# A sparse-attention and maxout-FFN kernel: the third output product of each half of the last FFN and the verdict's product use score tiles; the last product is made and stored in two column halves

## The chip, the cores and the metric

One core of one Trainium2 chip runs the program. The metric is the device time of one execution in microseconds; lower is better. Engine names are those of the profile: PE is the matrix engine's products, PEld its weight loads, DVE the vector engine, ACT the scalar engine, POOL the general-purpose engine, SP the engine whose queue issues most transfers. A "q" behind a name is that engine's sequencer or queue.

## The reference, cut to what matters

```python
# q, k, v: (4, 8, 768, 64); attention inside clusters, then a maxout FFN
mask   = q_assign[:, :, :, None] == k_assign[:, :, None, :]
attn   = softmax(where(mask, q @ k.T / sqrt(64), -1e9)) @ v
x      = attn.transpose(0, 2, 1, 3).reshape(3072, 512)
h      = maximum(maximum(x @ w1, x @ w2), x @ w3)      # 3072 x 768
return (h @ w_out).astype(float32)                     # 3072 x 512
```

## The kernel before, in words

There are 32 heads (4 batches of 8). Each head's tokens are sorted by cluster, its scores are made in blocks in a *score tile* (`big()`, line 69: two 512-column banks of the accumulator memory, in a pool of two buffers), its values in a *one-bank tile* (`one()`, line 72: 512 columns, a pool of two buffers), and the rows are gathered back into token order. The FFN of a batch of 768 tokens follows in two halves of 384 tokens (`ffn_units`, from line 923). A half has 18 hidden units (`hidden`, line 934), each 12 products of 384 columns into a one-bank tile at L941, evicted by ACT (L951) or DVE (L953), and after the third of a group cast by ACT (L957) and subtracted by DVE (L958) into a pair of 16-bit parts. Then come three output units (`outp(tt)`, tt = 0, 1, 2, line 963): 18 products of 512 columns at L974 into a one-bank tile, an eviction into an `o` tile of 128 x 512 (a tag `wd` of two buffers, line 982), and one store of it at L995 on SP's queue. In the last batch the eviction is by ACT for tt = 0 (L989), by DVE for tt = 1 (L987), and for tt = 2 ACT takes the left 256 columns (L992) and DVE the right 256 (L993), out of one bank.

The one-bank tiles are handed out to hidden units, output units, values and the verdict alike; score tiles to scores alone in the later batches. `judge` (line 1004) makes the verdict whether the sorted scheme may be used: some small vector operations, a product of 2 columns at L1015 into a one-bank tile, a reduction (L1017), a comparison (L1019), and `values_load` (L1020), which puts the flag into a register of every engine. At the program's end each engine branches on it (L1867): a second, general kernel runs only if the flag is set.

Order: every unit has a priority (its head number and an offset), `plan` lists the units by head, and the program is traced with `schedule_with_timeline_sim=True`: a planner orders each engine's queue by priority and by its own estimate of when operands are ready and buffers free. `judge` is put at priority `B * H - 0.5`, that is 31.5, the last scores at 31. The FFN of the last batch is traced last, all of its units with the same priority (`at_prio(B * H + 3, u)`). A queue executes in the order that the planner chose, and an instruction that waits holds up those behind it on its engine.

Of the kernel before, what the change touches and what calls it, by code (L numbers as in the profile page):

```python
# [14 lines left out]
AF = mybir.ActivationFunctionType  # L15
ALU = mybir.AluOpType
# [7 lines left out]
def sorted_attn__then__maxout_ffn(  # L24
# [17 lines left out]
    nc = tc.nc  # L42
    B, H, D, S = qk.shape
    D = D // 2
    C = cent.shape[0] // H
    P = 128
    QT = S // P
    NPAIR = H // 2
    DM = H * D
    DF = w1.shape[1]  # L50
    CT = DM // P
    JT = DF // P
    G = 3
    NB = G * P
    NG = QT // G
# [13 lines left out]
    def big():  # L69
        return ps_big.tile([P, 2 * 512], F32, tag="big", name="big")  # L70

    def one():
        return ps_one.tile([P, 512], F32, tag="one", name="one")

    def const(shape, dt, name):
        return cpool.tile(shape, dt, name=name)
# [7 lines left out]
    @contextmanager  # L84
    def behind(*made):
        with ExitStack() as s:
            for x in made:
                if x is not None:
                    s.enter_context(tc.issue_after(x.ins))
            yield  # L90
# [71 lines left out]
    for i, values in enumerate(SIDES.values()):  # L162
        x = 0
        while x < 4:
            n = 1
# [81 lines left out]
    wo16 = cpool.tile([P, JT, 2, DM], F16, name="wo16")  # L247
# [329 lines left out]
    def made(what, k):  # L577
        return st[k // H, k % H // 2][what, k & 1]
# [341 lines left out]
    HLS = ((0, 0), (0, 1), (1, 0))  # L920

    def ffn_units(b, gi):
        h16 = {}
        box = []
        tag = "wf" if gi else "vf"

        def slot(k):
            while len(box) <= k // 4:
                box.append(sb.tile([P, 4 * NB], F32, tag=tag, name=f"{tag}_h", bufs=2))
            return box[k // 4][:, k % 4 * NB : (k % 4 + 1) * NB]  # L930

        ms = {}

        def hidden(jt, i):
            def f():
                t = one()
                n = 0
                for ct in range(CT):
                    for xa, wa in HLS:
                        with behind(made("turn_pe", H - 1) if not (b or jt or i) else None):  # L940
                            nc.tensor.matmul(  # L941
                                t[:, 0:NB],
                                w16[:, jt, wa, i, ct],
                                x16[b, ct][:, xa * QT + gi * G : xa * QT + (gi + 1) * G, :],
                                start=(n == 0),
                                stop=(n == 3 * CT - 1),
                            )
                        n += 1
                m = slot(JT + (3 * jt + i) % 2)
                if i == 0:  # L950
                    nc.scalar.activation(m, t[:, 0:NB], AF.Copy, scale=2.0**-23)  # L951
                else:
                    nc.vector.scalar_tensor_tensor(m, t[:, 0:NB], 2.0**-23, ms[jt], op0=ALU.mult, op1=ALU.max)  # L953
                ms[jt] = m
                if i == 2:
                    x = slot(jt).bitcast(F16).rearrange("p (a n) -> p a n", a=2)
                    nc.scalar.copy(x[:, 0, :], m)  # L957
                    nc.vector.tensor_tensor(x[:, 1, :], m, x[:, 0, :], op=ALU.subtract)  # L958
                    h16[jt] = x

            return f

        def outp(tt):
            def f():
                if tt == 0:
                    so = ms["so"] = sb.tile([P, 1], F32, tag="so", name="so", bufs=3)
                    nc.vector.tensor_tensor(so, xsc[b][:, 0:1], wsc["w"], op=ALU.mult)
                    nc.vector.tensor_tensor(so, so, wsc["o"], op=ALU.mult)
                    nc.vector.tensor_scalar_mul(so, so, 2.0**9)
                t = one()  # L970
                n = 0
                for jt in range(JT):
                    for ha, wa in HLS:
                        nc.tensor.matmul(  # L974
                            t[:, 0:DM],
                            h16[jt][:, ha, tt * P : (tt + 1) * P],
                            wo16[:, jt, wa, :],
                            start=(n == 0),
                            stop=(n == 3 * JT - 1),
                        )  # L980
                        n += 1
                o = sb.tile([P, DM], F32, tag="wd", name="o", bufs=2)
                if b < B - 1:
                    nc.scalar.activation(o, t[:, 0:DM], AF.Copy, scale=ms["so"])
                elif tt < G - 1:
                    if tt & 1:
                        nc.vector.tensor_scalar(o, t[:, 0:DM], ms["so"], None, op0=ALU.mult)  # L987
                    else:
                        nc.scalar.activation(o, t[:, 0:DM], AF.Copy, scale=ms["so"])  # L989
                else:  # L990
                    h = DM // 2
                    nc.scalar.activation(o[:, 0:h], t[:, 0:h], AF.Copy, scale=ms["so"])  # L992
                    nc.vector.tensor_scalar(o[:, h:DM], t[:, h:DM], ms["so"], None, op0=ALU.mult)  # L993
                r = b * S + gi * NB + tt * P
                nc.sync.dma_start(out=out[r : r + P, :], in_=o)  # L995

            return f

        return [hidden(j, i) for j in range(JT) for i in range(3)] + [outp(tt) for tt in range(G)]
# [4 lines left out]
    def judge():  # L1004
        f = const([P, 2], F32, "flag_f")
        x = const([P, NH4], F32, "flag_x")
        v = nc.vector
        v.tensor_reduce(f[:, 0:1], n_off, axis=AX.X, op=ALU.max)
        v.tensor_scalar(x, n_key, float(C), None, op0=ALU.is_ge)
        v.scalar_tensor_tensor(x, n_own, 0.0, x, op0=ALU.is_equal, op1=ALU.mult)  # L1010
        v.tensor_reduce(f[:, 1:2], x, axis=AX.X, op=ALU.add)
        f16 = const([P, 2], F16, "flag_h")
        v.tensor_scalar(f16, f, 0.0, None, op0=ALU.is_gt)
        t = one()
        nc.tensor.matmul(t[0:1, 0:2], ones[:, 0:1], f16, start=True, stop=True)  # L1015
        r = const([1, 1], F32, "flag_r")
        v.tensor_reduce(r, t[0:1, 0:2], axis=AX.X, op=ALU.add)  # L1017
        bad = const([1, 1], I32, "bad")
        v.tensor_scalar(bad, r, 0.5, None, op0=ALU.is_ge)  # L1019
        verdict.append(nc.values_load(bad, min_val=0, max_val=1))  # L1020
# [15 lines left out]
    def when(p, k):  # L1036
        return p + AHEAD * max(0.0, 1.0 - (k - H) / H) if k >= H else p
# [3 lines left out]
    for b in range(B):  # L1041
        for hf in range(2):
            k = b * H + 4 * hf
            load, rest = four_units(b, hf)
            at = {H: 2, H + 4: H, 2 * H: H + 1}.get(k, max(k - 8, 0))
# [7 lines left out]
        for pr in range(NPAIR):  # L1053
            u = pair_units(b, pr)
            k = b * H + 2 * pr
            at = max(k - 5, 0)
            row_at = {H: 6, H + 2: 8, H + 4: 9, H + 6: 10}
            at = row_at.get(k, at)
            for x in u["load_rows"]:
                put(at, when(k - 5, k) - (k in (4, 6)), x)  # L1060
            at = max(k - 4, 0)
            at = row_at.get(k, at)
            for i, n in enumerate(("sums", "scales", "split_q")):
                put(at, when(k - 4 + 0.1 * i, k), u[n])
            for h in range(2):
                put(max(k + h - 4, at), when(k + h - 3.85, k), u["split_kv"][h])
                at, p = max(k + h - 2, 0), when(k + h - 2.5, k)
                if H <= k + h < H + 4:
                    at, p = H + 1, max(p, H + 0.7)
# [6 lines left out]
    for b in range(B):  # L1076
# [22 lines left out]
        if b + 1 < B:  # L1099
# [7 lines left out]
            units = hid + [u for x in units for u in x[3 * JT :]]  # L1107
            spread(units, k + 0.05, k + H, 0)
    put(B * H, B * H - 0.5, judge)
    spread(w_units(range(JT // 2)), 1, 6, 1)  # L1110
    spread(w_units(range(JT // 2, JT)), 9, 11.5, 0)
# [759 lines left out]
```

## Time and profile before

| | us |
|---|---|
| time before, median of 3 runs (lowest to highest) | 752.86 (752.25 to 754.35) |
| the profiled execution's own time | 747.1 |
| its span, first to last instruction | 745.3 |
| PE busy / DVE busy / ACT busy / POOL busy | 620.0 / 491.8 / 418.5 / 409.0 |

The profiled execution is 5.8 us below the median of the runs. The span starts at 0 and times in the rows count from there. The last FFN fills the stretch from about 642 us to the end; the verdict's product stands at 622.5 us. In a row of the timeline the first number is the start, the second the time from the first start to the last end of a run of like instructions, "x36" their count, and the bracket the idle time of the engine ahead of them with what ended it.

### The profile page before, as it was taken

To read this page: it belongs to the slowest core of one execution; us is meant where nothing else is said; L and a number is where in the kernel's file an instruction comes from. 1 tells how busy PE (TensorE), PEld (TensorE's weight loads), DVE (VectorE), ACT (ScalarE), POOL (GpSimd) and SP (SyncE) were. 2 spreads that over 40 slices of the span, in tenths; PEclk is the share of its full clock that TensorE was granted. 3 is DMA by queue.
4 is the path that set the end of the run, shared out by engine and by line. 5 is a ranking of instruction groups with operands and counts; after the bars stand their busy time and mean duration, and the time that the engine had idled before them with its cause. 6 is when DMAs were issued, how large, how long until landed. Compare 5 with 4: busy or idle time off the path is not lost.

```text
span 745.3 us, 12906 instructions
## 1 busy us (share of the span) xinstructions
PE 620.0 (83%) x4333; PEld 335.6 (45%) x4333; DVE 491.8 (66%) x1233; ACT 418.5 (56%) x1009; POOL 409.0 (55%) x426
## 2 busy tenths in 40 slices
PE   4556366467788986799999989998999999999995
PEld 1222233223444553365456555544555654564552
DVE  5898857779888999896759787853584532121220
ACT  5348978725869675666757578764565611211110
POOL 4576677735653777666664777766567555000000
PEclk8678878558899999999999999999999999999999
DMA  8864997889993995689785767665655644200001
GB/s 320 278 187 116 269 209 167 157 235 330 219 327 83 235 286 153 147 210 165 199 163 149 157 158 146 167 159 136 144 106 121 133 92 114 69 1 29 15 1 47
DMA packets 226908, 119.22 MB, mean 160 GB/s; under 512 B 196560, under 2 KB 205776, under 8 KB 226832
## 3 DMA queue, kind: packets, MB, share of 16 engines
q1 hardware_dynamic: 214928, 99.80, 54.5%
q0 software_dynamic: 11904, 18.50, 9.0%
q8 instruction: 36, 0.59, 0.3%
q14 instruction: 40, 0.33, 0.1%
HBM read 58.36 MB, written 28.84 MB: 117 GB/s over the span
## 4 chain that ended last, share of the span: by engine, by line
PE 42%; DMA 17%; issue 10%; POOL 10%; DVE 10%; ACT 9%; SPq 2%; DVEq 0%; POOLq 0%; ACTq 0%
PE one L941 22%; PE one L974 9%; POOL kv L692 6%; DMA pt<-hl 5%; POOL xb L848 4%; PE big L749 4%; DMA xb<-o,cl_idx 3%; ACT e L800 2%; DMA rows<-in_kr_dram 2%; DMA o<-of 1%; DVE kv L658 1%; DMA rows<-in_v_dram 1%; DVE hot L747 1%; DMA kv<-kv,cl_idx 1%; PE big L788 1%
## 5 line engine op out<-in xcount | busy, mean ns | idle before, releaser
L941 PE MATMUL one<-x,w 128*128 128x384 f16 x1728 | 296.8, 328 | 8.2 <-ACT wf_h L951 3.0
L692 POOL DMA_INDIRECT kv<-kv,cl_idx x192 | 206.9, 1077 | 115.8 <-issue 55.8
L848 POOL DMA_INDIRECT xb<-o,cl_idx x180 | 193.0, 1072 | 108.0 <-DMA o<-of 56.2
L941 PEld LDWEIGHTS <-w 128*128 128x128 f16 x1728 | 167.7, 98 | 122.9 <-issue 14.9
L749 PE MATMUL big<-hot,q 128*128 128x512 f16 x384 | 112.8, 410 | 30.2 <-DVE hot L747 20.4
L800 ACT ACTIVATE e<-big,nm,sc_al 128x128 f32<-128x128 f32 x256 | 113.4, 461 | 40.1 <-DVE nm L796 28.7
L747 DVE TENSOR_SCALAR hot<-line,cl_code 128x1024 f16<-128x1024 f16 x192 | 91.9, 500 | 12.8 <-PE big L749 12.4
L749 PEld LDWEIGHTS <-q 128*128 128x128 f16 x384 | 36.5, 103 | 75.4 <-issue 47.0
L953 DVE SCALAR_TENSOR_TENSOR vf_h<-one,vf_h 128x384 f32<-128x384 f32 x48 | 26.5, 552 | 48.6 <-PE one L941 46.8
L800 ACT ACTIVATION_READ_ACCUMULATOR e<-big,nm,sc_al 128x1 f32 x256 | 53.1, 208 | 0.0
L953 DVE SCALAR_TENSOR_TENSOR wf_h<-one,wf_h 128x384 f32<-128x384 f32 x48 | 26.5, 552 | 39.3 <-PE one L941 39.0
L974 PE MATMUL one<-wo,vf_h 128*128 128x512 f16 x216 | 48.3, 379 | 1.6 <-ACT o L989 1.1
L974 PE MATMUL one<-wo,wf_h 128*128 128x512 f16 x216 | 48.1, 379 | 0.8 <-ACT o L989 0.8
L825 PE MATMUL one<-vt,pt 128*128 128x64 f16 x256 | 29.1, 202 | 17.5 <-DMA pt<-hl 16.2
L757 ACT CAST qt<-big 128x1024 f16<-128x1024 f32 x32 | 32.3, 1010 | 17.6 <-PE big L749 17.3
L805 DVE SCALAR_TENSOR_TENSOR hl<-e,hl 128x1024 f16<-128x1024 f32 x32 | 38.9, 1214 | 2.7 <-ACT hl L804 2.4
L795 DVE TENSOR_REDUCE nm<-big 128x8 f32<-128x1024 f32 x32 | 38.9, 1215 | 1.4 <-PE big L791 1.2
L658 DVE SCALAR_TENSOR_TENSOR kv<-rows,sc_s,kv 128x384 f16<-128x384 f32 x64 | 37.4, 610 | 1.3 <-ACT kv L657 1.1
L657 ACT ACTIVATE kv<-rows,sc_s 128x384 f16<-128x384 f32 x64 | 35.7, 610 | 1.7 <-DVE sc_s L631 1.7
L957 ACT CAST vf_h<-vf_h 128x384 f16<-128x384 f32 x24 | 12.3, 513 | 43.1 <-DVE vf_h L953 43.0
L825 PEld LDWEIGHTS <-pt 128*128 128x128 f16 x256 | 24.7, 104 | 25.3 <-DMA pt<-hl 23.5
L830 DVE TENSOR_TENSOR of<-one,r 128x512 f32<-128x512 f32 x32 | 21.9, 684 | 20.9 <-PE one L827 16.5
(246 smaller groups left out, 910.9 us busy)
## 6 DMA issues: line engine op xcount, KB each, us to landing
stage<-in_qk_dram SPq DMA_DIRECT2D x32, 384.0 KB
wd<-in_moe_w_dram SPq DMA_DIRECT2D x18, 512.0 KB
vt<-kv SPq DMA_DIRECT2D x32, 256.0 KB
o<-of SPq DMA_DIRECT2D x30, 256.0 KB
rows<-in_qr_dram SPq DMA_DIRECT2D x16, 384.0 KB
rows<-in_kr_dram SPq DMA_DIRECT2D x16, 384.0 KB
rows<-in_v_dram SPq DMA_DIRECT2D x16, 384.0 KB
out_dram<-o SPq DMA_DIRECT2D x24, 256.0 KB
```

What stands on the lines that cost most here:

```text
L658: d["kv_lo", h] = nc.vector.scalar_tensor_tensor(kv[:, :, at + 1], x, s[:, i : i + 1], kv[:, :, at], op0=ALU.mult, op1=ALU.subtract)
L692: i = nc.gpsimd.indirect_dma_start(out=ring[at], out_offset=bass.IndirectOffsetOnAxis(ap=index(h, n, 1), axis=0), in_=d["kv", h][:, n].rea ...
L747: nc.vector.tensor_scalar(a, line, code, None, op0=ALU.is_equal)
L749: nc.tensor.matmul(t[:, lo : lo + 512], d["q16"][:, h * QT + n].rearrange("p a d -> p (a d)"), a[:, lo : lo + 512], start=(n == 0), stop=( ...
L795: d["max", i] = nc.vector.tensor_reduce(nm, ts, axis=AX.X, op=ALU.max)
L800: nc.scalar.activation(x[:, j], ts[:, j], AF.Exp, bias=nm[:, j : j + 1], scale=d["al"], accum_out=sm[:, j : j + 1])
L805: d["lo", i] = nc.vector.scalar_tensor_tensor(hl[:, 1], x, 2.0**14, hl[:, 0], op0=ALU.mult, op1=ALU.subtract)
L825: nc.tensor.matmul(o[:, j], pt[:, j], v[:, j, 0], start=True, stop=False)
L848: d["back", i] = nc.gpsimd.indirect_dma_start(out=d["x"][:, n, i * D : i * D + D], out_offset=None, in_=od, in_offset=bass.IndirectOffsetO ...
L941: nc.tensor.matmul(t[:, 0:NB], w16[:, jt, wa, i, ct], x16[b, ct][:, xa * QT + gi * G : xa * QT + (gi + 1) * G, :], start=(n == 0), stop=(n ...
L953: nc.vector.scalar_tensor_tensor(m, t[:, 0:NB], 2.0**-23, ms[jt], op0=ALU.mult, op1=ALU.max)
L974: nc.tensor.matmul(t[:, 0:DM], h16[jt][:, ha, tt * P : (tt + 1) * P], wo16[:, jt, wa, :], start=(n == 0), stop=(n == 3 * JT - 1),)
```

## The change

The third output unit of each half of the last FFN (b = 3, tt = 2) takes a score tile in place of a one-bank tile. In the second half (gi = 1) that unit is computed in two parts: 18 products of 256 columns into the first bank of the score tile, evicted and stored, and 18 of 256 columns into its second bank, evicted and stored. Both parts are evicted by ACT; the ACT/DVE split of the tt = 2 eviction is gone in both halves, so that the first half's third unit is one ACT eviction of 512 columns. The verdict's product takes a score tile.

```diff
-                t = one()
-                n = 0
-                for jt in range(JT):
-                    for ha, wa in HLS:
-                        nc.tensor.matmul(
-                            t[:, 0:DM],
-                            h16[jt][:, ha, tt * P : (tt + 1) * P],
-                            wo16[:, jt, wa, :],
-                            start=(n == 0),
-                            stop=(n == 3 * JT - 1),
-                        )
-                        n += 1
+                last = b == B - 1 and tt == G - 1
+                t = big() if last else one()
+                cuts = (0, DM // 2, DM) if last and gi == NG - 1 else (0, DM)
                 o = sb.tile([P, DM], F32, tag="wd", name="o", bufs=2)
-                if b < B - 1:
-                    nc.scalar.activation(o, t[:, 0:DM], AF.Copy, scale=ms["so"])
-                elif tt < G - 1:
-                    if tt & 1:
-                        nc.vector.tensor_scalar(o, t[:, 0:DM], ms["so"], None, op0=ALU.mult)
+                r = b * S + gi * NB + tt * P
+                for c, (lo, hi) in enumerate(zip(cuts, cuts[1:])):
+                    at = t[:, 512 * c : 512 * c + hi - lo]
+                    n = 0
+                    for jt in range(JT):
+                        for ha, wa in HLS:
+                            nc.tensor.matmul(
+                                at,
+                                h16[jt][:, ha, tt * P : (tt + 1) * P],
+                                wo16[:, jt, wa, lo:hi],
+                                start=(n == 0),
+                                stop=(n == 3 * JT - 1),
+                            )
+                            n += 1
+                    if b == B - 1 and tt & 1:
+                        nc.vector.tensor_scalar(o[:, lo:hi], at, ms["so"], None, op0=ALU.mult)
                     else:
-                        nc.scalar.activation(o, t[:, 0:DM], AF.Copy, scale=ms["so"])
-                else:
-                    h = DM // 2
-                    nc.scalar.activation(o[:, 0:h], t[:, 0:h], AF.Copy, scale=ms["so"])
-                    nc.vector.tensor_scalar(o[:, h:DM], t[:, h:DM], ms["so"], None, op0=ALU.mult)
-                r = b * S + gi * NB + tt * P
-                nc.sync.dma_start(out=out[r : r + P, :], in_=o)
+                        nc.scalar.activation(o[:, lo:hi], at, AF.Copy, scale=ms["so"])
+                    nc.sync.dma_start(out=out[r : r + P, lo:hi], in_=o[:, lo:hi])
...
-        t = one()
+        t = big()
         nc.tensor.matmul(t[0:1, 0:2], ones[:, 0:1], f16, start=True, stop=True)
```

## Rows read from the trace of the kernel before

**Rows 1.** The page: granted TensorE clock in 40 slices of the span.
```profile
PEclk8678878558899999999999999999999999999999
```

**Rows 2.** The chain that ended last, from 640 us: shares by line, one piece.
```profile
by line: PE one L941 66.2%; PE one L974 25.0%; ACT o L989 1.3%; issue 0.5%; ACT o L992 0.5%; DVE o L993 0.5%; ACTq L992 0.0%; ACTq L989 0.0%
...
733.73 0.70 ACT o L989
```

**Rows 3.** Timeline of PE, 677.7 to 739 us.
```profile
677.74 7.93 PE L974 MATMUL one<-wo,vf_h 128*128 128x512 f16 x36
686.78 4.04 PE L974 MATMUL one<-wo,vf_h 128*128 128x512 f16 x18 [1.11 <-ACT o L989]
...
725.76 7.93 PE L974 MATMUL one<-wo,wf_h 128*128 128x512 f16 x36
734.47 4.05 PE L974 MATMUL one<-wo,wf_h 128*128 128x512 f16 x18 [0.78 <-ACT o L989]
```

**Rows 4.** Timeline of DVE, ACT and SP's queue at the end.
```profile
733.09 0.75 DVE L987 TENSOR_SCALAR o<-one,so 128x512 f32<-128x512 f32 x1 [5.43 <-PE one L974]
...
738.60 0.47 ACT L992 ACTIVATE o<-one,so 128x256 f32<-128x256 f32 x1 [4.18 <-PE one L974]
739.11 0.48 DVE L993 TENSOR_SCALAR o<-one,so 128x256 f32<-128x256 f32 x1 [5.27 <-ACT o L992]
...
739.62 0.33 SPq L995 DMA_DIRECT2D out_dram<-o  x1
```

**Rows 5.** Timeline around the verdict, 621.4 to 623.4 us (PE, ACT, DVE).
```profile
621.58 0.19 PE L825 MATMUL one<-vt,pt 128*128 128x64 f16 x1
...
622.25 0.19 PE L827 MATMUL one<-vt,pt 128*128 128x64 f16 x1
622.51 0.16 PE L1015 MATMUL one<-flag_h,ones 128*1 128x2 f16 x1
...
621.77 0.69 ACT L984 ACTIVATE o<-one,so 128x512 f32<-128x512 f32 x1 [2.78 <-PE one L974]
...
623.08 0.14 DVE L1017 TENSOR_REDUCE flag_r<-one 1x1 f32<-1x2 f32 x1
```

**Rows 6.** Timeline of PE, 623.3 to 643 us.
```profile
623.22 7.93 PE L974 MATMUL one<-wo,vf_h 128*128 128x512 f16 x36 [0.54 <-DVE flag_r L1017]
630.99 11.82 PE L974 MATMUL one<-wo,wf_h 128*128 128x512 f16 x54
642.64 0.65 PE L941 MATMUL one<-x,w 128*128 128x384 f16 x3
```

**Rows 7.** Stretch: us, busy of PE, PEld, DVE, ACT, POOL, clock, DMA share, GB/s.
```profile
641.20:642.60 1.40, 1.40 (x8) 0.62 (x7) 0.00 (x0) 0.00 (x0) 0.00 (x0) 1.00 0.16 61
```

**Rows 8.** Instructions of line 974: duration ns minimum/median/maximum, first and last start.
```profile
L974 PEld LDWEIGHTS <-wf_h x216: 95/98/98, 358.4 to 737.9; 128*128 128x128 f16 x108
```

**Rows 9.** Instructions of line 992: ACT's wait ahead of its eviction.
```profile
L992 ACTq EVENT_SEMAPHORE  x2: 2067/2082/2098, 688.8 to 736.5; - x2
```

**Rows 10.** Instructions of line 1867: the branch at the program's end.
```profile
L1867 SPq EVENT_SEMAPHORE  x8: 17/17/17, 742.9 to 743.6; - x8
...
L1867 ACTq COMPARE_BRANCH  x1: 50/50/50, 739.2 to 739.2; - x1
...
L1867 SPq COMPARE_BRANCH  x1: 53/53/53, 740.0 to 740.0; - x1
L1867 ACTq EVENT_SEMAPHORE  x1: 17/17/17, 741.7 to 741.7; - x1
```

**Rows 11.** Stretches of the tail, columns as in rows 7.
```profile
740.00:741.00 1.00, 0.00 (x0) 0.00 (x0) 0.00 (x0) 0.00 (x0) 0.00 (x0) 1.00 0.60 213
...
742.00:743.00 1.00, 0.00 (x0) 0.00 (x0) 0.00 (x0) 0.00 (x0) 0.00 (x0) 0.50 0.07 20
```

**Rows 12.** Users of score tiles, columns as in rows 8: a head's maximum, its last eviction.
```profile
L800 ACT ACTIVATION_READ_ACCUMULATOR e<-big,nm,sc_al x256: 188/207/234, 57.4 to 592.6; 128x1 f32 x128
...
L795 DVE TENSOR_REDUCE nm<-big x32: 1204/1214/1225, 51.0 to 587.6; 128x8 f32<-128x1024 f32 x32
```

## The prediction

> **What bounds the kernel now.** The page comes first: PE runs at a granted clock of 0.9 or more in every slice of the later half [rows 1], so no step below changes the clock. The chain of waits from 640 us to the end comes second: 91% of it is PE at L941 and L974, and the rest is a few evictions [rows 2]. So in the last 100 us PE sets the time, and whatever holds PE up there is paid in full. The timeline of PE is third, read for brackets: there are three stops from 622 us on. Ahead of the third output unit of each half PE stands for 1.11 and 0.78 us until ACT has evicted the first unit [rows 3], and at 623.22 us it stands for 0.54 us after the verdict [rows 6]. All three are waits for a one-bank tile: two exist, and the third unit needs the one that tt = 0 still holds. The timeline of the end is fourth: behind the last product ACT and DVE work one after the other, 0.47 and 0.48 us, though each has its own columns, and the store follows [rows 4].
>
> **The change part by part.** *Verdict.* The 64-column products of the last head start at 621.58 and the last of the 24 at 622.25 [rows 5], 29 ns apart. Then the verdict's product waits until 622.51, just behind ACT's eviction, which ends at 621.77 + 0.69 = 622.46; the next output product waits until 623.22, when the reduction has ended (623.08 + 0.14) [rows 5, 6]. With the verdict in a score tile that product can take the tile that ACT freed at 622.46 and start at about 622.51: a gain of 0.71. Bounds: 0.54, the idle time that the row itself shows, and 0.94, if PE could go on right behind 622.25 + 0.03. I take 0.70, since the rotation of two tiles hands it the one that ACT freed. Is it passed on? PE is unbroken from 623.22 to 642.6: 36 and 54 products at 0.216 us, then the last FFN [rows 6]. That FFN needs the last gathered rows of x by its tenth product, over 1 us behind its start at 642.64 (three take 0.65 [rows 6]); the transfers have ended by 642.6, and the share of 0.16 in that stretch puts their end nearer to 641.4 [rows 7]. So at least 1.0 us covers a shift of 0.70. What moves with the verdict: the reduction, the comparison and the flag's loads on five queues; on SP a load may now wait earlier, behind nothing but a store that has 4 us of slack, and I cost it at nothing. Were SP's cover gone, the price is a store late by half a microsecond, which nothing waits for.
>
> *Third unit of the first half.* Its 18 products would follow the 36 in step. Those start at 677.74, 36 x 0.216 = 7.77, so the next could issue at 685.51 in place of 686.78 [rows 3]: a gain of 1.27 (the row's idle time, 1.11, is the lower bound, since it counts from a product's modelled end). The next hidden unit then takes the one-bank tile that tt = 0 gives back, with 3.9 us of products as cover for an eviction of 0.70. The eviction becomes one ACT instruction of about 0.70 where two of 0.47 and 0.48 stood; no product waits for that tile, so nothing is paid.
>
> *Third unit of the second half.* By the same sum 725.76 + 7.77 = 733.53 against 734.47 [rows 3]: a gain of 0.94, at least 0.78.
>
> *Two halves of columns.* 18 products of 512 columns become 36 of 256, with 18 more weight loads. A step of 512 columns takes 0.216, one of 64 takes 0.029 [rows 3, 5]; on that line 256 columns take 0.109, and 36 of them 3.92 against 3.88: a loss of 0.04. The weight loads last 98 ns [rows 8] and were hidden even behind steps of 29 ns, so I cost them at nothing; if the cover went, a pair would cost 98 + 109 = 207 ns. [...]
>
> *The end.* The left half is evicted while PE makes the right half (18 x 0.109 = 1.96 us), so only ACT's 0.47 stands behind the last product; the store issues 739.11 - 738.60 = 0.51 earlier [rows 4]. The left eviction needs an `o` buffer, and before it was free only at 736.5, when the store of tt = 0 had landed [rows 9]: 2.0 us behind that eviction's end. Shifted with the rest, it ends 0.7 us before the right half is due, so this wait is hidden too. SP issues one more store, 0.33 us, inside the same 1.96 us.
>
> *Behind the last store.* 745.27 - 739.62 = 5.65 us remain: SP branches at 740.0 and goes on at 742.9, where ACT took 739.2 to 741.7 [rows 10], 2.9 against 2.5 us. The store's data flow mostly in 740 to 741, with a rest in 742 to 743 [rows 11]. The last store is now half as large, and DVE no longer branches in the same moment. No row has the smaller store; the gain is bounded by 0.6 (SP as quick as ACT, plus 0.2 of the store) and by a loss of 0.3 (the rest of the store later still). I take 0.10, near nothing, because SP's own branch stays.
>
> Sum: 0.70 + 1.27 + 0.94 - 0.04 + 0.51 + 0.10 = 3.48. Against the profiled execution, 747.1, that is 743.6; the median of the runs is 5.8 us (0.8%) above that execution, and no row tells where; I take the gain to be the same in both, so I subtract from the median: 752.86 - 3.48 = **749.4**. The bounds of the terms give gains of 2.5 to 4.3, thus 748.6 to 750.4.
>
> **The rivals.** *The stop moves in the first half (0.15).* All units of the last FFN have one priority, and the planner already puts tt = 1 (18 products) ahead of the last 3 of tt = 0: DVE's eviction starts 0.64 us before ACT's [rows 2, 4]. With the third unit free to start, it may come ahead of those 3 as well; then the next hidden unit meets tt = 0's eviction and stands where the third unit stood. The 1.27 is lost: a gain of 2.2, 750.7. For it speaks that order; against it that either of two tiles will do.
>
> *The halves are not free of each other (0.07).* If the planner holds the right half until the left half's eviction has read the tile, PE stops for that eviction. It cannot start before the `o` buffer is free, about 1 us after the left half is made, and takes 0.47: a gain of 3.48 - 1.5 = 2.0, 750.9. For it: ACT and DVE on different columns of one tile do wait for each other [rows 4]. Against it: there they share a bank, here not. In this case the change doesn't do what its halves are for.
>
> *Weight loads show (0.02).* 36 x 0.207 = 7.45 against 3.88, 3.6 us: no gain, 752.9. Rows 5 and 8 speak against it.
>
> *The verdict takes a score tile while scores still need it (0.06).* This one ends slower. The verdict's operands are ready long before its product, and score tiles are two; a product placed among the heads holds one until its reduction, which stands in DVE's queue. From the start of a head's maximum on DVE to the tile's release it is 592.8 - 587.6 = 5.2 us [rows 12], and the head that is displaced loses about that; with the reduction behind two operations of a head on DVE like that maximum, 1.2 us each, some 2.4 more. The price is 7.6, the outcome 752.86 - 3.5 + 7.6 = 757.0. It decides from a delay of 3.5 us. Against it: its priority is behind the last scores, and score tiles lie unused from 593 us on, 30 us before the verdict's present place.
>
> *More than forecast (0.06).* If the branch at the end is quicker by a whole microsecond, the gain is 4.5 and the time 748.4.
>
> **How the numbers follow.** The forecast has the remaining 0.64. A measurement tells 0.3%, 2.26 us, from no change, so the border is 750.6. Faster: the forecast, the larger gain and a third of the moved stop, 0.64 + 0.06 + 0.05 = 0.75. Same: the rest of the moved stop, the bound halves and the weight loads, 0.10 + 0.07 + 0.02 = 0.19. Slower: 0.06. The range reaches from 748.0, past the low end of the forecast's bounds, to 751.2, past the bound halves; the slower case and the weight loads stay outside, with some of the larger gains.
>
> **What would show it.** Right: no bracket ahead of the third unit's products in either half; 0.109 us per product of 256 columns; the verdict's product reads a score tile and the output product behind it starts about 0.05 us after ACT's eviction; one ACT eviction of 0.47 between the last product and the last store; the last store issued about 3.4 us earlier in the span (736.2). Wrong: a stop of about 1 us ahead of the first hidden unit of the second half; a gap between the 18th and the 19th product of 256 columns; a verdict product before 593 us with score products waiting behind it; a step near 0.2 us in the halves; more than 5.7 us from the last store to the end.

## The result, and the profile after

| | before | after |
|---|---|---|
| median of 20 runs each, us | 751.12 (746.05 to 755.26) | 755.06 (750.72 to 759.95) |
| the profiled execution: own time, span, us | 747.1, 745.3 | 753.23, 751.4 |
| first product of the last FFN to the end of the span, us | 102.63 | 107.01 |
| last value product to first product of the last FFN, us | 20.40 | 19.69 |

After divided by before is 1.0056 [1.0034, 1.0077]: the changed kernel is slower by 0.0056 x 751.1 = 4.2 us. The forecast was 3.5 us less, with a chance of 0.06 on slower. Ratios compare the runs of the chip's undisturbed state alone, so that a ratio can differ a little from that of two medians.

The timeline of PE in the last FFN comes first, beside [rows 3]. Of rows that repeat only the first stand here.

```profile
644.36 9.91 PE L941 MATMUL one<-x,w 128*128 128x384 f16 x60
654.11 0.81 PE L980 MATMUL big<-wo,vf_h 128*128 128x512 f16 x3
654.75 6.01 PE L941 MATMUL one<-x,w 128*128 128x384 f16 x36
...
690.25 1.03 PE L980 MATMUL one<-wo,vf_h 128*128 128x512 f16 x4
692.38 9.91 PE L941 MATMUL one<-x,w 128*128 128x384 f16 x60 [1.10 <-ACT o L991]
702.13 0.49 PE L980 MATMUL big<-wo,wf_h 128*128 128x256 f16 x3
...
736.24 0.27 PE L980 MATMUL big<-wo,wf_h 128*128 128x256 f16 x1
736.35 1.03 PE L980 MATMUL one<-wo,wf_h 128*128 128x512 f16 x4
741.03 4.00 PE L980 MATMUL big<-wo,wf_h 128*128 128x256 f16 x18 [3.65 <-ACT o L991]
```

A *stop* is a time in which PE runs nothing, because its next product waits. The third output unit no longer stands behind the other two. Its products come three at a time among the hidden units, as each pair of 16-bit parts gets ready (654.11, 702.13). So the last PE work before the second half is one of the units with a one-bank tile, and the next hidden unit meets its eviction: 1.10 us. In the second half only the left columns are done early. The 18 products of the right columns wait 3.65 us and then take 4.00 us, 0.213 each, where 256 columns cost 0.109 in the left half. The timeline of the end, beside [rows 4], tells what they wait for:

```profile
736.77 0.75 DVE L989 TENSOR_SCALAR o<-one,so 128x512 f32<-128x512 f32 x1 [5.75 <-PE one L980]
737.41 0.69 ACT L991 ACTIVATE o<-one,so 128x512 f32<-128x512 f32 x1 [6.99 <-PE one L980]
738.12 7.77 SPq L992 DMA_DIRECT2D out_dram<-o  x4
740.50 0.47 ACT L991 ACTIVATE o<-big,so 128x256 f32<-128x256 f32 x1 [2.40 <-DMA out_dram<-o]
741.03 4.00 PE L980 MATMUL big<-wo,wf_h 128*128 128x256 f16 x18 [3.65 <-ACT o L991]
...
745.07 0.47 ACT L991 ACTIVATE o<-big,so 128x256 f32<-128x256 f32 x1 [4.09 <-PE big L980]
```

The chain of waits names the same pieces, in order of time (start, length, what):

```profile
738.12 2.29 DMA out_dram<-o
...
740.50 0.48 ACT o L991
...
741.03 4.01 PE big L980 x18
```

The left half is complete about 736.5 us. Its eviction needs an `o` buffer, and both are taken: the first unit's is evicted at 737.41, stored at 738.12, and free when that store has *landed*, that is, when its end is signalled to the waiting engine, 2.3 us later. Only behind the left half's eviction do the right half's products start, though they write another bank of the tile. Windows of the trace (length, busy time of PE, PEld, DVE, ACT and POOL, clock, DMA share, GB/s) show what the stop costs besides:

```profile
735.00:737.20 2.20, 2.20 (x13) 1.12 (x12) 0.43 (x1) 0.00 (x0) 0.00 (x0) 1.00 0.00 0
737.20:741.00 3.80, 0.17 (x1) 0.00 (x0) 0.32 (x1) 1.16 (x2) 0.00 (x0) 0.79 0.37 140
742.00:743.00 1.00, 1.00 (x7) 0.68 (x5) 0.00 (x0) 0.00 (x0) 0.00 (x0) 0.50 0.31 100
```

The granted clock is 1.00 while PE works ahead of the stop, 0.79 in the mean from 737.20 to 741.00 us, which holds the stop, and 0.50 in the products behind it.

Here the difference of the two stretches is added up. Stops are counted from start to start of products, since brackets count from modelled ends: in the first half the stop is 1.48 us before and after, so 0. In the second it was 1.16 and is 4.03, so +2.87. The clock adds 18 x (0.213 - 0.109) = 1.87, the 36 products of 256 columns in place of 18 of 512 add 0.04. From the last eviction's start to the last store it is 0.50 in place of 1.02, so -0.52. From the last store to the end 5.80 in place of 5.65, +0.15. Together 4.41; measured 107.01 - 102.63 = 4.38.

The verdict, beside [rows 5, 6]:

```profile
585.31 0.16 PE L1012 MATMUL big<-flag_h,ones 128*1 128x2 f16 x1
586.14 0.10 DVE L1014 TENSOR_REDUCE flag_r<-big 1x1 f32<-1x2 f32 x1
589.59 0.22 PE L791 MATMUL big<-high,qt 64*128 64x128 f16 x1
...
624.67 0.19 PE L827 MATMUL one<-vt,pt 128*128 128x64 f16 x1
624.93 7.93 PE L980 MATMUL one<-wo,vf_h 128*128 128x512 f16 x36
```

It moved ahead of the last head's scores, and its stop is gone: from the last value product to the next output product 0.26 us where it was 0.97, a gain of 0.71. The two pieces give 4.38 - 0.71 = 3.67 us, a ratio of 1.0049, inside the measured interval. The spans of the two profiles differ by 6.1; the other 2.4 us lie ahead of the last value product (622.25 and 624.67). A second profile of the unchanged kernel has that product at 629.46, and two profiles of the best kernel below have it at 627.76 and 626.16, so this place shifts by microseconds with no change at all. Why is open. The stretches behind it are what the experiments below are compared by.

### The profile page after: what moved, and what is told of

Same layout as the page of the kernel before. It is cut to its first block, busy times and chain, and to the rows that moved or that the text cites. A ratio compares the mean times of both kernels' runs of the same rounds, so it can differ in the third digit from the quotient of the medians.

```text
span 751.4 us, 12941 instructions
## 1 busy us (share of the span) xinstructions
PE 624.7 (83%) x4351; PEld 340.0 (45%) x4351; DVE 489.3 (65%) x1231; ACT 418.8 (56%) x1010; POOL 412.3 (55%) x426
## 4 chain that ended last, share of the span: by engine, by line
PE 43%; DVE 17%; DMA 17%; issue 8%; ACT 7%; POOL 5%; SPq 1%; DVEq 0%; ACTq 0%; POOLq 0%
PE one L941 23%; PE one L980 8%; PE big L749 5%; DMA pt<-hl 4%; POOL xb L848 3%; POOL kv L692 2%; DVE hot L747 2%; ACT e L800 2%; DMA kv<-kv,cl_idx 2%; DMA wd<-in_moe_w_dram 2%; DMA o<-of 2%; DVE kv L658 2%; DMA xb<-o,cl_idx 2%; DMA rows<-in_v_dram 2%; PE big L980 1%
## 5 line engine op out<-in xcount | busy, mean ns | idle before, releaser
L941 PE MATMUL one<-x,w 128*128 128x384 f16 x1728 | 300.6, 330 | 9.9 <-ACT wf_h L951 3.2
L692 POOL DMA_INDIRECT kv<-kv,cl_idx x192 | 211.1, 1099 | 114.7 <-issue 54.5
L980 PE MATMUL one<-wo,vf_h 128*128 128x512 f16 x198 | 44.7, 379 | 0.1
L980 PE MATMUL one<-wo,wf_h 128*128 128x512 f16 x198 | 44.4, 379 | 0.0
L991 ACT ACTIVATE o<-one,so 128x512 f32<-128x512 f32 x20 | 13.7, 686 | 42.8 <-PE one L980 36.8
L980 PEld LDWEIGHTS <-wf_h 128*128 128x128 f16 x234 | 23.6, 101 | 28.5 <-issue 3.9
```

The source lines that it names most:

```text
L692: i = nc.gpsimd.indirect_dma_start(out=ring[at], out_offset=bass.IndirectOffsetOnAxis(ap=index(h, n, 1), axis=0), in_=d["kv", h][:, n].rea ...
L941: nc.tensor.matmul(t[:, 0:NB], w16[:, jt, wa, i, ct], x16[b, ct][:, xa * QT + gi * G : xa * QT + (gi + 1) * G, :], start=(n == 0), stop=(n ...
L980: nc.tensor.matmul(at, h16[jt][:, ha, tt * P : (tt + 1) * P], wo16[:, jt, wa, lo:hi], start=(n == 0), stop=(n == 3 * JT - 1),)
```

## The experiments

*Stretch* is the time from the first product of the last FFN to the end of the span, 102.63 us before. The forecast's own steps for it, without the verdict's 0.70, come to 102.63 - 2.78 = 99.85. Diffs are against the changed kernel unless another is named; `behind(x)` puts an instruction behind x in its queue's order.

**The order of the third unit.** Its products are put behind those of the first two units, in both halves.

```diff
+                    with behind(*(ms["ends"] if last else ())):
                         ... the product loops, with mm = nc.tensor.matmul(
+                    ms.setdefault("ends", []).append(mm)
```

> The changed kernel with one thing added: the products of the third unit are issued behind the last products of the first two units, in both halves. Measure: the stretch from the first product of the last FFN to the end of the span, 102.6 us before, 107.0 in the changed kernel. Theory (the planner spread the third unit among the hidden units, which moved the first half's stop to the next hidden unit; and the right half of columns shares a tile with the left half, so it waits for the left half's eviction, which waits for an o buffer): the 1.1 us stop ahead of the second half's hidden units is gone; the left half follows the first two units in step; the right half stands until the left half's eviction has ended, about 3.7 us behind the end of the first two units, less 1.96 us of the left half's own products, a stop of about 1.8 us. Stretch 101.7 us if the granted clock holds over that stop, 103.6 if it falls and the right half takes 3.9 us instead of 1.96. Rival (the stop ahead of the right half came from the spread alone): no stop, stretch 99.9 us.

Measured: stretch 101.97, ratio 0.9984 [0.9956, 1.0011].

```profile
736.98 2.13 PE L981 MATMUL big<-wo,wf_h 128*128 128x256 f16 x18
740.18 0.47 ACT L993 ACTIVATE o<-big,so 128x256 f32<-128x256 f32 x1 [2.31 <-DMA out_dram<-o]
740.70 2.13 PE L981 MATMUL big<-wo,wf_h 128*128 128x256 f16 x18 [1.59 <-ACT o L993]
```

```profile
739.00:740.70 1.70, 0.11 (x1) 0.00 (x0) 0.00 (x0) 0.47 (x1) 0.00 (x0) 1.00 0.66 249
740.70:742.80 2.10, 2.10 (x18) 1.65 (x17) 0.00 (x0) 0.00 (x0) 0.00 (x0) 1.00 0.23 74
```

Order alone gives back 107.01 - 101.97 = 5.04 us. The first half's stop behind the output units is gone. The stop between the column halves is still there, since the eviction waits for the same landing, but the left half's products now fill part of it: 1.59 us in place of 3.65. Behind this shorter stop the clock is 1.00 and the step 0.109. So the slow products of the changed kernel belong to the long stop, not to their shape or to their place at the end.

**The tile of the right half, in that order.** The same, and the right columns get a score tile of their own.

```diff
-                    at = t[:, 512 * c : 512 * c + hi - lo]
+                    t = big() if c else t
+                    at = t[:, 0 : hi - lo]
```

> As the run before, and the right half of columns has a score tile of its own. This is the kernel that the prediction had in mind. Theory: no stop in either half, 36 products of 256 columns in 3.9 us, stretch from the first product of the last FFN to the end 99.9 us (99.4 to 100.5), 2.7 us less than before, so a ratio to before of about 0.996 with the verdict's part. Rival (products of 256 columns take 0.2 us each because weight loads show): 36 of them take 7.5 us, stretch 103.5 us.

Measured: stretch 100.46, ratio 0.9962 [0.9933, 0.9990].

```profile
696.67 31.36 PE L941 MATMUL one<-x,w 128*128 128x384 f16 x192 [0.42 <-ACT wf_h L951]
...
735.63 4.09 PE L982 MATMUL big<-wo,wf_h 128*128 128x256 f16 x36
738.72 0.47 ACT L994 ACTIVATE o<-big,so 128x256 f32<-128x256 f32 x1 [2.20 <-DMA out_dram<-o]
739.77 0.47 ACT L994 ACTIVATE o<-big,so 128x256 f32<-128x256 f32 x1 [0.57 <-PE big L982]
```

The 36 products of the two halves are one unbroken run of 4.09 us. The left eviction still waits 2.20 us for the landing, and nothing waits for it: this is the picture that the forecast had. Two banks of one tile were therefore one thing to the program's dependencies (a stop of 1.59 us), and two tiles are two (none). A stop of 0.42 is left at 696.67, behind the first 24 hidden products of the second half: ACT's first eviction of them starts only at 696.13, when all 24 are nearly done, as it would if the planner had mixed the two units. The best version below, which puts them in order, has no such stop.

**The `o` buffer.** In the changed kernel's own order, the third unit's `o` comes from another tag.

```diff
-                o = sb.tile([P, DM], F32, tag="wd", name="o", bufs=2)
+                o = sb.tile([P, DM], F32, tag="e" if last else "wd", name="o", bufs=2)
```

> The changed kernel, with o buffers of another tag for the third unit, so that its eviction waits for no store. Theory: the planner still spreads the third unit, the first half's stop stays at about 1.1 us ahead of the next hidden unit; the left half's eviction comes first on ACT and ends before the first two units do, so the right half follows with no stop (at most 0.2 us), at full clock, in 1.96 us. Stretch 101.2 us against 107.0. Rival (the o buffer isn't what held it): the stop of 3.6 us stays and so does 107.

Measured: stretch 101.19, ratio 0.9983 [0.9952, 1.0015].

```profile
735.76 0.47 ACT L991 ACTIVATE o<-big,so 128x256 f32<-128x256 f32 x1 [6.13 <-PE big L980]
736.42 2.13 PE L980 MATMUL big<-wo,wf_h 128*128 128x256 f16 x18
736.67 0.69 ACT L991 ACTIVATE o<-one,so 128x512 f32<-128x512 f32 x1 [0.44 <-PE one L980]
738.59 0.47 ACT L991 ACTIVATE o<-big,so 128x256 f32<-128x256 f32 x1 [1.23 <-PE big L980]
```

PE behind the first half, and SP's issues of line 992 (duration in ns: minimum, median, maximum; first and last start):

```profile
691.59 9.91 PE L941 MATMUL one<-x,w 128*128 128x384 f16 x60 [0.82 <-ACT o L991]
...
L992 SPq DMA_DIRECT2D out_dram<-o x25: 332/356/1669, 353.2 to 739.6; - x25
```

One tag takes away 107.01 - 101.19 = 5.82 us. The left eviction comes first, at 735.76, and the right half follows its neighbours without a stop, 18 products in 2.13 us, a step of 0.109. The expected 101.2 was met in part by luck: the moved stop of the first half is 0.82 here, not 1.10, and the last store is issued 1.0 us behind the start of the last eviction in place of 0.5, since the store ahead of it took SP 1.67 us to issue (the longest of the 25).

**The tile alone, order and buffer as in the change.** The two tile lines above, and nothing else.

> The changed kernel, with a score tile of its own for the right half of columns and nothing else. Theory (the right half waited only because it shares a tile with the left half): both halves are spread among the hidden units, PE has no stop in the second half and no fall of the clock; the first half's stop of 1.1 us ahead of the next hidden unit stays; but the left half's eviction still waits for the store of the first unit, 2.3 us, with the right half's eviction queued behind it on ACT. Stretch about 104.4 us: 2.6 less than the changed kernel, 1.8 more than before. Rival (the halves depend on each other in another way): the stop of 3.6 us and 107 stay.

Measured: stretch 106.26, 1.9 us more than the 104.4 expected, ratio 1.0040 [1.0010, 1.0070].

```profile
738.81 5.82 SPq L993 DMA_DIRECT2D out_dram<-o  x4
...
743.33 0.84 ACT L992 ACTIVATE o<-big,so 128x256 f32<-128x256 f32 x2 [4.54 <-DMA out_dram<-o]
```

```profile
740.00:741.00 1.00, 0.00 (x0) 0.00 (x0) 0.00 (x0) 0.00 (x0) 0.00 (x0) 1.00 0.94 361
741.00:742.00 1.00, 0.00 (x0) 0.00 (x0) 0.00 (x0) 0.00 (x0) 0.00 (x0) 0.83 0.08 18
742.00:743.00 1.00, 0.00 (x0) 0.00 (x0) 0.00 (x0) 0.00 (x0) 0.00 (x0) 0.50 0.06 18
```

PE has no stop here. The landing is simply what the end waits for, and it took 4.5 us in place of 2.3: most of the data flowed in one microsecond, the rest at a share of 0.08 and 0.06, about one engine of 16. Around it the engines reach the program's end: PE's branch starts at 735.6 and takes 3.6 us, DVE branches at 738.1 and goes on at 741.0 (instructions of line 1865), and the view of the DMA queues from 738 to 745 us has two queues of the kind instruction (packets, MB, share of 16 engines):

```profile
L1865 PEldq COMPARE_BRANCH  x1: 3597/3597/3597, 735.6 to 735.6; - x1
L1865 DVEq COMPARE_BRANCH  x1: 72/72/72, 738.1 to 738.1; - x1
...
L1865 DVEq EVENT_SEMAPHORE  x1: 21/21/21, 741.0 to 741.0; - x1
```

```profile
q8 instruction: 1, 0.02, 1.6%
q14 instruction: 3, 0.02, 1.4%
```

That these transfers hold up the rest of the store would fit the rows; no run takes them away, so it stays the author's guess. If one does, it is the one on q8. In the changed kernel DVE branches as long ahead of the same store, 0.7 us (737.4 and 738.12), and a transfer on q14 falls into its landing too, yet that took 2.3 us; none on q8 does (queues from 738.12 to 740.50 us).

**No column halves.** Two kernels leave the last unit whole: one with `cuts = (0, DM)`, one with the third unit's own `o` tag besides. "The run before" in the first text is the second kernel.

> As the run before, but with the o buffers of the changed kernel (two for all units). Theory: the third unit's eviction waits on ACT for the landing of the first unit's store, behind the last product: 2.3 us as in the changed kernel, or up to 4.5 as in the run with two tiles, and 0.7 of eviction. Stretch 104.2 us, up to 106.4: no gain and no fall of the clock, a loss made by the o buffer alone. Rival (the buffer wait is hidden): 101.2 us as in the run before.

> The changed kernel without the halves of columns (18 products of 512 into the score tile in both halves of the FFN) and with o buffers of another tag for the third unit. Theory: the planner spreads the third unit; the first half's stop of 1.1 us stays; the second half has no stop, its last products are those of the first unit, and one eviction of 0.69 us stands behind them: stretch 101.2 us, about 1.4 less than before. So the halves are worth at most a few tenths. Rival (without the halves the end is worse than before): over 102.6.

Measured: stretch 104.93, ratio 1.0041 [1.0012, 1.0071], and stretch 103.05, ratio 1.0004 [0.9978, 1.0029]. The first kernel's end:

```profile
739.50 0.69 ACT L991 ACTIVATE o<-one,so 128x512 f32<-128x512 f32 x1 [7.31 <-PE one L980]
...
743.25 0.69 ACT L991 ACTIVATE o<-big,so 128x512 f32<-128x512 f32 x1 [3.06 <-DMA out_dram<-o]
```

Without halves PE never stops in the second half, and the wait for the landing is paid once, by ACT at the very end. So 104.93 - 102.63 = 2.3 us of the loss stand with no column halves at all, and the halves add 107.01 - 104.93 = 2.1. That is near what the clock takes (1.87), but this landing took 3.0 us (issued at 740.22), 0.7 more than in the changed kernel, so the two sums can't be set against each other to a few tenths. The second kernel missed its number by 1.9 us, behind the last store:

```profile
742.45 3.28 SPq L992 DMA_DIRECT2D out_dram<-o  x3
...
L992 SPq DMA_DIRECT2D out_dram<-o x24: 332/390/1944, 356.3 to 743.8; - x24
```

The third of its three stores took SP 1.94 us to issue, where the median of the 24 is 0.39, and the span ends 7.17 us behind that issue's start (5.80 in the changed kernel): 1.4 of the 1.9 us lie there. Three stores of 128 x 512 are issued within 1.4 us of each other; no run parts that from the branches (739.1 to 745.8 us) and the transfers of the kind instruction (q14 seven, q8 one, from 743 to 751 us) that go on beside them.

**The verdict alone, and the kernel before once more.** The first is the kernel before with `t = big()` in `judge`, the second that kernel with no edit.

> The kernel before with one part of the change alone: the verdict's product writes a score tile. Theory (it only closes the stop behind the last values): from the last value product of the last head to the first product of the last FFN 19.7 us instead of 20.4; the stretch of the last FFN stays 102.6; time 0.7 us less, ratio about 0.999. Rival (standing among the last heads it holds a score tile and delays them): the same 0.7 us gained there, and several microseconds lost ahead of it, ratio over 1.002.

> The kernel before, unchanged, as a control. Its queues hold the same instructions in the same order as those of the kernel with the verdict's part alone, up to the verdict's product near 585 us. Theory (what differs between profiles ahead of that product is one execution against another): the last score product of the last head, at 587.2 us in the first profile, falls anywhere between 587 and 593 here, and the last-FFN stretch is 102.6 us again (within 0.2); ratio 1.000. Rival (the changed kernels are late ahead of the verdict for a cause of their own): the last score product at 587.2 within 0.5 again.

Measured: with the verdict alone 19.69 us from values to the FFN, stretch 102.53, ratio 1.0014 [0.9988, 1.0039]. The kernel before again: 20.40 and 102.53, and a ratio of 0.9955 [0.9916, 0.9993] to itself (medians of all runs 752.47 and 751.65, which differ by 0.1%). Of this kernel the stretches repeat to 0.1 us; a single ratio near half a per cent settles nothing here. The 0.71 is thus shown where it arises, and is too small for the ratio. A price of the verdict among the heads would lie ahead of both stretches, so they can't show one. The last score product of the last head can: with the verdict in a one-bank tile it starts at 587.18 (before), 594.10 (before again, just past the 593 expected) and 592.16 (`e11_verdict_back`, below), with the score tile at 589.59 (the changed kernel), 592.82 (the verdict alone), and 590.88 and 589.21 (the best version, twice). No delay shows; one of a microsecond or two would be lost in the spread.

**The best version.** The order and the two tiles, and the hidden units of the last FFN each behind the one before; run twice, and once with the verdict back in a one-bank tile (`t = one()`).

```diff
-                        with behind(made("turn_pe", H - 1) if not (b or jt or i) else None):
-                            nc.tensor.matmul(
+                        with behind(made("turn_pe", H - 1) if not (b or jt or i) else None, ms.get("hid") if b == B - 1 else None):
+                            mm = nc.tensor.matmul(
...
+                ms["hid"] = mm
```

> The kernel with third units in order and two tiles, and each hidden unit of the last FFN issued behind the one before it. Theory (the 0.6 us stop that was left, ahead of the third hidden unit of the second half, comes from the planner's mixing the first two hidden units, so that both tiles come free together): 12 products after 12, no stop, stretch 99.9 us instead of 100.46, ratio to before about 0.995. Rival (the stop is ACT's, behind the one eviction of 512 columns): the stop of 0.6 us stays.

> The kernel with the last FFN wholly in order and two tiles, with the verdict's product back in a one-bank tile. Theory (the verdict's part is worth 0.7 us and nothing else): 20.4 us from the last value product to the last FFN instead of 19.7, the stretch 99.7 us as there, the time 0.7 us above the run beside it: ratio to before near 0.996. Rival (the verdict's move costs more among the heads than it brings): faster than the run beside it by over 1 us, ratio 0.994 or less.

> The kernel with the last FFN wholly in order, two tiles and the verdict in a score tile, a second time, beside the run with the verdict back. Theory: 2.9 us from the last FFN and 0.7 from the verdict, 3.6 in all, ratio to before 0.995 (measured before: 0.9968 with an interval from 0.9942 to 0.9993). Rival: as for the run beside it, ratio over 0.997.

Measured, in this order: stretch 99.67, 99.43 and 100.07; values to FFN 19.69, 20.40 and 19.69; medians 748.19, 748.08 and 747.38; ratios 0.9968 [0.9942, 0.9993], 0.9962 [0.9936, 0.9988] and 0.9952 [0.9923, 0.9982]. PE of the first:

```profile
694.21 35.26 PE L941 MATMUL one<-x,w 128*128 128x384 f16 x216
729.31 7.93 PE L983 MATMUL one<-wo,wf_h 128*128 128x512 f16 x36
737.08 4.09 PE L983 MATMUL big<-wo,wf_h 128*128 128x256 f16 x36
```

No bracket is left. The three stretches differ by what lies behind the last store, 5.41, 5.18 and 5.82 us. The 0.71 comes and goes with the verdict's tile, and the medians of the last two kernels differ by the 0.70 expected, though that is within their noise. By both stretches together the gains over the kernel before are 3.67, 3.20 and 3.27 us (102.63 - 99.67 + 0.71 for the first), 0.4 to 0.5%, and the three intervals agree; since the interval of the unchanged kernel against itself lies below 1 as well, this rests on the stretches and not on the ratios. Against the changed kernel it is nearly 1%. Among themselves the three can't be told apart.

## Why the prediction was wrong

**The step that failed** is "Its 18 products would follow the 36 in step", used for both halves. It took the queue's order of before and removed one wait. But the wait for a one-bank tile had made that order: with a score tile free, the third unit was as ready as any hidden unit of the same priority, and the planner spread it. With the order put back and two tiles, the stretch was 100.46, with the hidden units in order too 99.67, around the forecast's 99.85. Order alone gave back 5.04 of the 107.01 - 99.85 = 7.16 us between forecast and measurement. So the terms were right for an order that the change does not produce.

**The first half.** The forecast gave 1.27; it was 0. The rival of the moved stop described it, though by a smaller shift than the one that came: the whole third unit moved, where three products were thought of. Its chance of 0.15 was far too low: with the third unit spread, both one-bank tiles are held at the end of the half, and the next hidden unit needs one of them.

**The second half.** "so this wait is hidden too" assumed that the left half is made last, behind the first unit's eviction. Made early, it has nothing to do during the landing, and the right half depends on it. The rival that the halves are not free of each other named this wait, with 1.5 us for it; it took 2.87 more than the old stop, because the whole landing stood open. The argument against it, that the halves lie in different banks, was false: one tile [e1] gave a stop of 1.59, two tiles [e6] none.

**The clock.** "so no step below changes the clock" failed with it, for 1.87 us. Without the long stop it held: the clock was 1.00 behind the stop of 1.59 us [e1], and the step stayed at 0.109 us where there was none [e6]. The forecast read the clock of before [rows 1] as given, and priced a stop at its length only.

**How the rivals were joined.** Each was priced alone, and each alone left a gain. They have one cause, the new order, and so they came together: 1.27 + 0.94 of gain not made, and 2.87 + 1.87 of loss on top. The rival that was given the side of slower, the verdict among the scores, happened as to place (585.31), but PE, ACT and DVE run the heads' work in the order of before, and the last score product shows none of its 7.6 us.

**Right:** the verdict's gain, 0.71 for 0.70; 0.109 us for a product of 256 columns; the end with one eviction, 0.52 for 0.51; weight loads hidden. On the last: behind the stop of [e1] 18 products take 2.10 us with 17 weight loads of 1.65 us in all beside them, 97 ns each, where one after the other they would take 18 x 0.109 + 1.65 = 3.61; and 36 products ran unbroken in 4.09 us [e6], where the rival had 7.45. Behind the last store the forecast had -0.10, measured was +0.15, inside its bounds. The bounds of the terms add up to gains of 2.6 to 4.2, not 2.5 to 4.3; nothing hangs on that.

## What to carry to other kernels

A wait for a buffer also fixes an order; whoever takes it away must work out which order a planner will choose next, or write the order down, as the last kernels here did, with a gain of some 3 us over the kernel before. Two parts of one tile were tied to each other here even in different banks, so parts that are to overlap are better given tiles of their own. And the stop of 3.65 us cost here, besides its length, what the clock took from the work behind it, 1.87 us, while behind the one of 1.59 us the step stayed at 0.109.

## What was not expected of the hardware

The granted clock fell to 0.50 in a stop of 3.65 us and stayed at 1.00 over one of 1.59 us. The first unit's store of 128 x 512 landed 2.2 to 2.4 us after its issue in the changed kernel and in the kernels in order, 3.0 us in the kernel without halves and 4.5 us in the one with two tiles, there with a slow rest at a DMA share of 0.06 to 0.08. In that kernel q8 and q14 move one and three packets of the kind instruction from 738 to 745 us, and DVE goes on 2.9 us behind its branch (738.1 to 741.0); in the changed kernel q14 moves one during the landing and q8 none, and DVE goes on 3.1 us behind its branch (737.4 to 740.5). Whether the transfer on q8 made the slow rest no run here shows.
